# Six transposes of x in a chunked linear-attention and MLP kernel: from DMA to TensorE, with fewer unread matmuls

## The chip, the cores and the metric

The kernel runs on one core of a Trainium2 chip. The metric is device time in microseconds (us) of one execution; for the kernel before it is the median of six executions. A further execution was recorded by the hardware profiler, and all rows shown come from that one.

The engines are named as in the profile: PE (TensorE matmuls), PEld (TensorE weight loads), DVE (VectorE), ACT (ScalarE), POOL (GpSimd) and SP (SyncE, which here only issues DMAs). Each engine works through its own queue in order.

## The reference, cut to what matters

```python
# q, k, v: (4, 8, 768, 64); lam: (8,)
for b in range(nb):                       # blocks of 64 rows
    intra = (qb @ kb.T * Dmask) @ vb      # Dmask[i, j] = lam ** (i - j) for i >= j
    inter = (qb * lam_pow) @ kv_state
    out[block] = intra + inter
    kv_state = lam ** 64 * kv_state + (kb * rev_pow).T @ vb
x = out as (4, 768, 512)                  # the heads side by side
xn = (x - mean) / sqrt(var + 1e-6) * g_ln
result = x + relu(xn @ w_ch1) @ w_ch2     # 512 -> 2048 -> 512
```

Attention with a decay per head and a running state per batch and head, then a normalised two-layer MLP with a residual.

## The kernel before, in words

**Tiles.** The 4 x 768 rows are cut into 12 pairs `u` of two 128-row chunks (`ab` = 0, 1). Pair `u` belongs to batch `u % 4`, so a batch's state passes from pair `u` to pair `u + 4`. The code counts from 0: the "pairs 4 to 6" of the change are `u` = 3, 4, 5, and the "third group" is `g` = 2. Pairs 0 to 5 use `scores`, `kv`, `av`; pairs from 6 on use `scores64`, `kv64`, `av64`, which work in blocks of 64 rows. The MLP works on groups `g`, one per pair, so 256 rows at a time.

**Stages of a pair.** Loads of k, q, v (SP); scaling and casting into `kq` and `vb` (`in_k_one`, `in_q_one`, `in_v`, mostly on POOL); a DMA transpose of `kq` to `kqT` (`transpose_dma`, line 266); scores and masked scores (PE line 282 or 362, DVE line 292 or 368); the state (`kv`, `new_state`, `states64`); the products of masked scores with v (`av`, line 428, or `av64`, line 415); the inter-chunk products (`inter`, line 441), which add to the same two PSUM banks `po0` and `po1`. Halfway through `inter`, `reader` makes DVE (for pairs up to 6) read eight columns of each bank into `seen` (line 452), and the second half of `inter` waits for that.

**From x to the MLP.** `norm(u, ab)` copies x out of `po` (ACT, line 463), takes mean and variance (DVE, lines 465 and 466), and writes the centred and scaled bf16 tile `xc` (DVE, line 470). `to_xT(u, ab)` makes its transpose, a half of the group's `xT`: for pairs 0 and 1 by four PE transposes into a bank of the pool `mm` and an ACT copy (lines 490 and 491), for all others by a DMA transpose on SP's queue (line 486). `rstd_of` makes 1/std (ACT line 496, DVE line 498), which is applied at the very end.

**Units of the MLP.** The MLP is cut into units. An `m1` unit is 8 matmuls of 128x256 (line 530) and one ACT relu of 128x512 into `hT` (line 533). An `m2` unit of groups 0 to 5 is 4 matmuls of 128x512 (line 666); a quarter of a chunk's output, and every fourth is followed by the output's DVE instruction (line 690). For groups 6 to 11 the second layer is done by seven products of half-sized blocks instead of eight (line 565), for which `w_sums` makes sums of weights on DVE (lines 787 to 791). The units lie in one list, `plan`, in order of groups; `units(n)` takes the next n.

**What sets the order.** Nothing is scheduled by a planner: the last 350 lines of the kernel write the order out by hand, attention steps between units, and every engine's queue follows that order. The scheduler that the language offers is switched off (`manual_schedule`), and only semaphores for data and buffers are added.

**PSUM.** All eight banks are given away: four to `mm`, two to `sc`, one each to `po0` and `po1`. A new tile in a bank waits until all readers of the one before it are done.

**Unread matmuls.** In the first `m1` unit of group 2, 20 matmuls of 128x8 into the unit's own bank come first; the unit's real matmuls overwrite them (lines 525 and 526).

```python
        if u >= 2:
            nc.sync.dma_start_transpose(dst, s["xc"][:, ab])
        else:
            xt = mm_tile([128, KA, 128], BF16, "xt")
            for kk in range(KA):
                nc.tensor.transpose(xt[:, kk, :], s["xc"][:, ab, kk * 128:(kk + 1) * 128], ident)
            nc.scalar.copy(dst, xt)
```

Of the kernel before, what the change touches and what calls it, by code (L numbers as in the profile page):

```python
# [8 lines left out]
BF16 = mybir.dt.bfloat16  # L9
# [8 lines left out]
def kernel(  # L18
# [20 lines left out]
    KA = DM // 128  # L39
# [15 lines left out]
    ps = ctx.enter_context(tc.tile_pool(name="ps", bufs=1, space=PSUM))  # L55

    half = [slice(0, 64), slice(64, 128)]
    XB = 3
    LB = 6

    def mm_tile(shape, dtype, name):
        return ps.tile(shape, dtype, tag="mm", bufs=4, name=name)
# [4 lines left out]
    def source(src, u, hs):  # L67
        cc, b = divmod(u, B)
        return src[b, hs, cc * W:(cc + 1) * W, :].rearrange("h (p j) d -> p h (j d)", j=2)

    def fill(got, name, u, hs, eng=None):
        eng = eng or nc.sync
        src = dict(k=k, q=q, v=v)[name]
        if u < LB:
            eng.dma_start(got[:, hs], source(src, u, hs))  # L75
# [11 lines left out]
    def open_in(u, gate):  # L87
        qkv_in[u] = {name: inp.tile([128, H, 2 * D], F32, tag=name + "in", name=name + "in") for name in "kqv"}
        if gate:
            nc.gpsimd.memset(qkv_in[u]["k"][:, 0, 0:1], 0.0)  # L90

    def load_in(u, name, eng):
        got = qkv_in[u][name]
        fill(got, name, u, slice(0, H), eng)
        qkv_in[u][name] = got.rearrange("p h (j d) -> p h j d", j=2)
# [54 lines left out]
    def make_keep64():  # L150
        for dst, base in ((keep64, 0), (keep64_b, D)):
            nc.gpsimd.memset(dst, 1.0)
            nc.gpsimd.affine_select(
                out=dst, in_=dst, compare_op=ALU.is_ge, fill=0.0,
                base=base, pattern=[[1, D]], channel_multiplier=-1,
            )
        nc.vector.tensor_copy(keep64[half[1]], keep64_b[half[1]])
# [49 lines left out]
    def open_window(u):  # L207
        kq = wk.tile([128, 2, NP, 2, 2, D], BF16, tag="kq", bufs=3, name="kq")
        vb = wk.tile([128, H, 2, D], BF16, tag="vb", bufs=4, name="vb")
        st[u] = dict(kq=kq, vb=vb)  # L210
        if u < XB:
            st[u]["kqT"] = wk.tile([128, 2, NP, 2, 128], BF16, tag="kqT", bufs=3, name="kqT")

    def part(a, dst, hs):

        return dst[:, a, hs.start // 2:hs.stop // 2].rearrange("p a j e d -> p a e j d")
# [9 lines left out]
    def in_q(u, eng, hs=ALL):  # L226
        src = qkv_in[u]["q"][:, hs].rearrange("p (a e) j d -> p a e j d", e=2)
        dst = part(1, st[u]["kq"], hs)
        if u < LB:
            lq = lam_q[:, hs, :].rearrange("p (a e) j -> p a e j", e=2)  # L230
# [11 lines left out]
    def in_q_one(u, eng, j):  # L242
        src = qkv_in[u]["q"].rearrange("p (a e) j d -> p a e j d", e=2)
        lq = (lam_q[:, :, j] if u < LB else lam_p[:, 0, :]).rearrange("p (a e) -> p a e", e=2)
        eng.tensor_tensor(part(1, st[u]["kq"], ALL)[:, :, :, j], src[:, :, :, j],  # L245
                          lq[:, :, :, None].to_broadcast([128, NP, 2, D]), op=ALU.mult)

    def in_v(u, eng, hs=ALL):
        n = hs.stop - hs.start
        lv = lam_v[:, hs, :, None] if u < LB else lam_p[:, 1, hs, None, None]  # L250
        eng.tensor_tensor(st[u]["vb"][:, hs], qkv_in[u]["v"][:, hs], lv.to_broadcast([128, n, 2, D]), op=ALU.mult)  # L251
# [167 lines left out]
    def av(u, pairs, chunks=(0, 1)):  # L419
        s = st[u]  # L420
        if "po" not in s:
            s["po"] = [ps.tile([128, H, D], F32, tag=f"po{ab}", name=f"po{ab}") for ab in range(2)]
        for p in pairs:
            for e in range(2):
                for j in range(2):
                    for jq in range(2):
                        for ab in chunks:
                            nc.tensor.matmul(s["po"][ab][half[jq], 2 * p + e, :],  # L428
                                             lhsT=s[f"mA{p // 2}"][half[ab], e, p % 2, j, half[jq]],
                                             rhs=s["vb"][half[ab], 2 * p + e, j],  # L430
                                             start=(p == 0 and e == 0 and j == 0), stop=False, skip_group_check=True)
# [45 lines left out]
    def to_xT(u, ab):  # L477
        s = st[u]
        t = 2 * u + ab
        g = group_of[t]  # L480
        i = t - groups[g][0]
        if i == 0:
            xT_of[g] = gp.tile([128, KA, GT * 128], BF16, tag="xT", bufs=3, name="xT")
        dst = xT_of[g][:, :, i * 128:(i + 1) * 128]
        if u >= 2:
            nc.sync.dma_start_transpose(dst, s["xc"][:, ab])
        else:
            xt = mm_tile([128, KA, 128], BF16, "xt")
            for kk in range(KA):
                nc.tensor.transpose(xt[:, kk, :], s["xc"][:, ab, kk * 128:(kk + 1) * 128], ident)  # L490
            nc.scalar.copy(dst, xt)

    def rstd_of(u):
        s = st[u]
        std = wk.tile([128, 2], F32, tag="std", name="std")
        nc.scalar.activation(std, s["mv"][:, :, 1], ACT.Sqrt, bias=eps_t, scale=XS * XS)
        rstd = xp.tile([128, 2], F32, tag="rstd", name="rstd")
        nc.vector.reciprocal(rstd, std)
        x_keep[u] = (s["x"], rstd)
# [13 lines left out]
    def mlp(g):  # L513
# [6 lines left out]
        def m1(u):  # L520
            nonlocal hT
            if hT is None:
                hT = gp.tile([128, KB, GT * 128], F16, tag="hT", bufs=2, name="hT")
            pm = mm_tile([128, NB, N], F32, "pm1")
            for _ in range(20 if (g, u) == (2, 0) else 0):
                nc.tensor.matmul(pm[0:8, 0, 0:8], lhsT=fill_in, rhs=fill_in, start=True, stop=True, skip_group_check=True)
            for b in range(NB):
                n = u * NB + b
                for kk in range(KA):
                    nc.tensor.matmul(pm[:, b, :], lhsT=w1[n // W2K][:, kk, (n % W2K) * 128:(n % W2K + 1) * 128],  # L530
                                     rhs=xT_of[g][:, kk, 0:N], start=(b == 0 and kk == 0),
                                     stop=(b == NB - 1 and kk == KA - 1), skip_group_check=True)
            nc.scalar.activation(hT[:, u * NB:(u + 1) * NB, 0:N], pm, ACT.Relu)  # L533
# [138 lines left out]
        m2.sums = h_sums  # L672
        m2s[g] = m2
        return m1, m2

    def rows_of(u):

        cc, b = divmod(u, B)
        order = "(c p j) d -> j p c d" if u < LB else "(j c p) d -> j p c d"
        return out[b, cc * W:(cc + 1) * W, :].rearrange(order, c=2, j=2)  # L680
# [15 lines left out]
    def store(u):  # L696
        for j in range(2):
            nc.sync.dma_start(rows_of(u)[j], o_of[u][half[j]])
# [82 lines left out]
    def w_sums(c, n):  # L781
        v = w2[c].rearrange("p (k e) d -> p k e d", e=2)
        w = DM // 2
        b11, b12, b21, b22 = v[:, :, 0, 0:w], v[:, :, 0, w:], v[:, :, 1, 0:w], v[:, :, 1, w:]
        t1, t2, t3, t4 = (wt[c][:, :, i] for i in range(4))
        if n == 0:
            nc.vector.tensor_tensor(t1, b12, b11, op=ALU.subtract)
            nc.vector.tensor_tensor(t3, b12, b22, op=ALU.add)
        else:
            nc.vector.tensor_tensor(t2, b11, t3, op=ALU.subtract)  # L790
            nc.vector.tensor_tensor(t4, t2, b21, op=ALU.add)
# [28 lines left out]
    def s1(u):  # L820
        kv(u)
        scores(u, 0)
        new_state(u, 0, nc.gpsimd)
        mask(u, 0, (0,))
        new_state(u, 1, nc.gpsimd)
        mask(u, 0, (1,))

    def wind_up(u):


        s = st[u]
        if u < LB:
            av(u, range(NP))
# [45 lines left out]
    def s4(u):  # L879
        inter(u, 1)  # L880
        if st[u]["S"][0][1] is not None:
            norm(u, 0)
        norm(u, 1)

    def p4(u):
        to_xT(u, 0)
        to_xT(u, 1)
# [27 lines left out]
    def X2(u):  # L915
        scores64(u)
        inter(u - 1, 1)
        mask64(u, 0)
        norm(u - 1, 0)
        norm(u - 1, 1)  # L920
        mask64(u, 1)

    def X(u):

        if u - 1 < LB:
            av(u - 1, range(NP))
        else:
            av64(u - 1)
        inter(u - 1, 0)
        kv64(u)  # L930
        scores64(u)
        inter(u - 1, 1)
        states64(u, 0)
        mask64(u, 0)
        states64(u, 1)
        norm(u - 1, 0)
        norm(u - 1, 1)
        mask64(u, 1)
# [89 lines left out]
    def units(n):  # L1028
        for _ in range(n):
            f, *a = next(steps)  # L1030
            f(*a)
# [60 lines left out]
    s3(3)  # L1092
    units(1)
    s4(3)
    to_xT(3, 0)
    to_xT(3, 1)
    open_in(6, False)
    load_in(6, "k", nc.sync)
    units(1)
# [3 lines left out]
    units(2)  # L1103
    rstd_of(3)
    make_keep64()
    units(3)
    store(2)
    transpose_dma(5, 0)
    transpose_dma(5, 1)
# [14 lines left out]
    s3(4)  # L1124
    units(2)
    s4(4)
    to_xT(4, 0)
    to_xT(4, 1)
    load_in(7, "q", nc.sync)
    units(2)  # L1130
    transpose_dma(6, 0)
    transpose_dma(6, 1)
    load_in(7, "v", nc.sync)
    units(4)
    s1(5)
    rstd_of(4)
    open_window(7)
# [16 lines left out]
    load_in(8, "k", nc.sync)  # L1154
    units(2)
    X2(6)
    to_xT(5, 0)
    to_xT(5, 1)
    in_v(7, nc.gpsimd)
    load_in(8, "q", nc.sync)  # L1160
    load_in(8, "v", nc.sync)
# [5 lines left out]
    w_sums(1, 0)  # L1167
    rstd_of(5)
    units(1)
    w_sums(1, 1)  # L1170
    units(4)
    X(7)
    store(4)
# [166 lines left out]
```

## Time and profile before

| What | us |
|---|---|
| median of six executions | 212.37 |
| lowest and highest of them | 211.62 and 214.89 |
| the profiled execution's own time | 213.04 |
| its span, from its first to its last instruction | 211.3 |
| PE busy in the span | 199.7 |
| DVE, ACT, POOL busy | 139.6, 98.0, 83.2 |
| share of the 16 DMA engines' span on the queue that SP fills | 74.3% |

The span of 211.3 us and the 1.7 us around it make the profiled execution's 213.04 us. All positions below are us from the span's start. Rows of instruction groups give line, engine, operation, the tiles written and read (out<-in), the count, then busy time and the mean duration of one. The duration of a matmul is longer than the distance to the next one's start, since matmuls overlap in the array; where the text counts PE time, it takes distances between starts.

### The profile page before, as it was taken

The numbers are of one execution on the slowest core, as the hardware profiler recorded it, in microseconds if no ns is written. First come the engines' busy times: TensorE is split into PE (matmuls) and PEld (weight loads), VectorE is DVE, ScalarE is ACT, GpSimd is POOL, SyncE is SP. The second block draws the span as 40 slices with busy tenths as digits, with TensorE's granted clock in tenths as the row PEclk, the third lists the DMA queues.
The fourth block names the chain that finished last, engine by engine and source line by source line (L and its number), as shares of the span: only waits on it lengthen the run. The fifth ranks groups of instructions, "written<-read, shape, count | busy, mean of one in ns | idle before, by whom it ended". The sixth has DMA issues, their size and how long they took to land.

```text
span 211.3 us, 7148 instructions
## 1 busy us (share of the span) xinstructions
PE 199.7 (94%) x3079; PEld 151.2 (72%) x3079; DVE 139.6 (66%) x293; ACT 98.0 (46%) x195; POOL 83.2 (39%) x113
## 2 busy tenths in 40 slices
PE   2988997999999999999999999999999999999992
PEld 1477786644685476487477488888888888888881
DVE  2577652448556464755997589899797887876253
ACT  3855878411154055237057067185284372661630
POOL 4647318519837174208237055273192202011020
PEclk9999999999999999999999999999999999999998
DMA  3999999999999999999989899898948950430303
GB/s 104 299 270 214 167 245 192 201 305 287 172 296 269 131 228 205 177 175 247 203 187 243 152 225 150 173 199 145 163 76 165 285 128 3 103 50 0 99 16 87
DMA packets 94305, 37.17 MB, mean 176 GB/s; under 512 B 68417, under 2 KB 91457, under 8 KB 94274
## 3 DMA queue, kind: packets, MB, share of 16 engines
q1 hardware_dynamic: 89664, 32.32, 74.3%
q0 software_dynamic: 4224, 4.19, 12.7%
q8 instruction: 24, 0.39, 0.8%
q10 hardware_dynamic: 386, 0.20, 0.4%
q14 instruction: 7, 0.06, 0.1%
HBM read 27.27 MB, written 6.29 MB: 159 GB/s over the span
## 4 chain that ended last, share of the span: by engine, by line
PE 61%; issue 13%; DMA 13%; DVE 5%; POOL 3%; SPq 2%; ACT 1%; POOLq 0%; DVEq 0%; ACTq 0%
PE pm L530 28%; PE pm L666 17%; DMA w<-in_moe_w_ch_dram 5%; DMA qin<-in_q_dram 4%; PE pwa L565 3%; DMA kin<-in_k_dram 3%; PE pwd L565 2%; PE pwc L565 2%; SPq L75 2%; PE po L441 1%; PE sc L282 1%; PE pwb L565 1%; PE po L428 1%; POOL o L590 1%; POOL kq L245 1%
## 5 line engine op out<-in xcount | busy, mean ns | idle before, releaser
L530 PE MATMUL pm<-xT,w 128*128 128x256 bf16 x736 | 85.0, 273 | 0.1
L530 PEld LDWEIGHTS <-w 128*128 128x128 bf16 x736 | 70.0, 98 | 9.6 <-issue 0.6
L533 ACT ACTIVATE hT<-pm 128x512 f16<-128x512 f32 x92 | 55.1, 599 | 40.1 <-PE pm L530 39.4
L666 PE MATMUL pm<-w,hT 128*128 128x512 f16 x192 | 43.3, 379 | 0.0
L666 PEld LDWEIGHTS <-hT 128*128 128x128 f16 x192 | 18.2, 98 | 20.5
L322 POOL TENSOR_TENSOR Sn<-Stmp,lam_s 128x256 bf16<-128x256 f32 x16 | 9.8, 612 | 53.4 <-DVE Stmp L400 34.6
L565 PEld LDWEIGHTS <-hs 128*128 128x128 f16 x192 | 18.7, 98 | 2.2
L292 DVE TENSOR_TENSOR mA<-sc,keep 128x512 bf16<-128x512 f32 x20 | 13.1, 682 | 8.3 <-PE sc L282 8.3
L470 DVE SCALAR_TENSOR_TENSOR xc<-po,mv,g_row 128x512 bf16<-128x512 f32 (+1 forms) x24 | 16.8, 706 | 1.8
L463 ACT COPY x<-po 128x512 f32<-128x512 f32 x18 | 9.9, 588 | 15.7 <-PE po L441 10.4
L565 PEld LDWEIGHTS <-hT 128*128 128x128 f16 x144 | 13.6, 98 | 2.7 <-ACT hT L533 1.2
L590 POOL TENSOR_TENSOR o<-ev_u,x 128x256 f32<-128x256 f32 x4 | 3.1, 782 | 31.5 <-ACT ev_u L589 31.5
L548 DVE TENSOR_TENSOR hs<-hT 128x1024 f16<-128x1024 f16 x12 | 10.4, 865 | 6.9 <-ACT hT L533 6.9
L465 DVE BATCH_NORM_STATS2 stats<-x 128x6 f32<-128x512 f32 x18 | 12.4, 686 | 3.8 <-ACT x L463 3.7
L245 POOL TENSOR_TENSOR kq<-qin,lam_q 128x512 bf16<-128x512 f32 x10 | 10.3, 1045 | 8.1 <-DMA qin<-in_q_dram 8.1
L690 DVE SCALAR_TENSOR_TENSOR o<-pm,rstd,x 128x512 f32<-128x512 f32 x12 | 8.8, 743 | 6.9 <-PE pm L666 6.9
L251 POOL TENSOR_TENSOR vb<-vin,lam_v 128x1024 bf16<-128x1024 f32 (+1 forms) x7 | 11.6, 1660 | 2.5 <-DMA vin<-in_v_dram 1.6
L251 POOL TENSOR_TENSOR vb<-vin,lam_p 128x1024 bf16<-128x1024 f32 x6 | 11.4, 1897 | 2.8 <-DMA vin<-in_v_dram 2.7
L245 POOL TENSOR_TENSOR kq<-qin,lam_p 128x512 bf16<-128x512 f32 x12 | 12.3, 1042 | 0.2
L452 ACT COPY seen<-po 128x8 f32<-128x8 f32 x8 | 1.0, 166 | 17.5 <-PE po L441 17.5
L368 DVE TENSOR_TENSOR mA<-sc,keep 128x512 bf16<-128x512 f32 x12 | 8.2, 680 | 1.4 <-PE sc L362 1.4
L259 PE MATMUL tp<-ident,kq 128*128 128x128 bf16 x48 | 6.2, 265 | 1.7 <-DVE kq L240 0.8
(139 smaller groups left out, 265.4 us busy)
## 6 DMA issues: line engine op xcount, KB each, us to landing
out_dram<-o SPq DMA_DIRECT2D x18, 256.0 KB, 4.9
w<-in_moe_w_ch_dram POOLq DMA_DIRECT2D x8, 512.0 KB, 9.1
kin<-in_k_dram SPq DMA_DIRECT2D x14, 256.0 KB, 4.9
qin<-in_q_dram SPq DMA_DIRECT2D x14, 256.0 KB, 4.7
vin<-in_v_dram SPq DMA_DIRECT2D x14, 256.0 KB, 5.2
kin<-in_k_dram SPq DMA_DIRECT2D x5, 512.0 KB, 7.1
qin<-in_q_dram SPq DMA_DIRECT2D x5, 512.0 KB, 9.1
vin<-in_v_dram SPq DMA_DIRECT2D x5, 512.0 KB, 8.7
```

The source lines that it names most:

```text
L245: eng.tensor_tensor(part(1, st[u]["kq"], ALL)[:, :, :, j], src[:, :, :, j], lq[:, :, :, None].to_broadcast([128, NP, 2, D]), op=ALU.mult)
L251: eng.tensor_tensor(st[u]["vb"][:, hs], qkv_in[u]["v"][:, hs], lv.to_broadcast([128, n, 2, D]), op=ALU.mult)
L292: nc.vector.tensor_tensor(s[f"mA{hf}"][:, e], s[f"sc{hf}"][e], kp[:, None, :, :].to_broadcast([128, 2, 2, 128]), op=ALU.mult)
L322: eng.tensor_tensor(dst, src, lam_s[:, :, None].to_broadcast([128, NP, D]), op=ALU.mult)
L463: nc.scalar.copy(x, po)
L465: nc.vector.bn_stats(stats, po if early else x)
L470: nc.vector.scalar_tensor_tensor(xc[:, sl], in0=po[:, sl], scalar=mv[:, 0:1], in1=g_row[:, sl], op0=ALU.subtract, op1=ALU.mult)
L530: nc.tensor.matmul(pm[:, b, :], lhsT=w1[n // W2K][:, kk, (n % W2K) * 128:(n % W2K + 1) * 128], rhs=xT_of[g][:, kk, 0:N], start=(b == 0 and ...
L533: nc.scalar.activation(hT[:, u * NB:(u + 1) * NB, 0:N], pm, ACT.Relu)
L548: nc.vector.tensor_tensor(s13, b[:, :, 1:2, :].to_broadcast([128, n, 2, 128]), b[:, :, 0:4:3, :], op=ALU.subtract)
L565: nc.tensor.matmul(pr[bank], lhsT=lhs(r), rhs=rhs, start=(first and r == 0), stop=(r == KB // 2 - 1), skip_group_check=True)
L666: nc.tensor.matmul(acc[i], lhsT=hT[:, kk, i * 128:(i + 1) * 128], rhs=w2[kk // W2K][:, kk % W2K, :], start=(kk == 0), stop=(kk == KB - 1))
```

## The change

Three things change.

1. `to_xT` for `u` = 3, 4, 5 no longer issues a DMA transpose on SP. It makes four PE transposes into a bf16 tile that takes the bank `po{ab}` (the bank of the same pair's `av` and `inter` products, free once `norm` has read it), and an ACT copy from there to `xT`.
2. The calls of `to_xT` for these pairs move to later places in the hand-written order. For `u` = 3 they go from just behind `s4(3)` to places with four and five more units ahead of them; for `u` = 4 the same, with four and five units of the six that lie between `s4(4)` and `s1(5)`; for `u` = 5 both go behind the fifth of nine units between `X2(6)` and `X(7)`, with `w_sums(1, 1)` between them.
3. The unread matmuls ahead of group 2 go from 20 to 4.

```diff
     XB = 3
+    X_PE = (3, 4, 5)
     LB = 6
...
-        if u >= 2:
+        if u >= 2 and u not in X_PE:
             nc.sync.dma_start_transpose(dst, s["xc"][:, ab])
         else:
-            xt = mm_tile([128, KA, 128], BF16, "xt")
+            if u < 2:
+                xt = mm_tile([128, KA, 128], BF16, "xt")
+            else:
+                xt = ps.tile([128, KA, 128], BF16, tag=f"po{ab}", name="xt")
             for kk in range(KA):
                 nc.tensor.transpose(xt[:, kk, :], s["xc"][:, ab, kk * 128:(kk + 1) * 128], ident)
             nc.scalar.copy(dst, xt)
...
-            for _ in range(20 if (g, u) == (2, 0) else 0):
+            for _ in range(4 if (g, u) == (2, 0) else 0):
...
     s4(3)
-    to_xT(3, 0)
-    to_xT(3, 1)
     open_in(6, False)
     load_in(6, "k", nc.sync)
     units(1)
...
     make_keep64()
-    units(3)
+    to_xT(3, 0)
+    units(1)
+    to_xT(3, 1)
+    units(2)
     store(2)
...
     s4(4)
-    to_xT(4, 0)
-    to_xT(4, 1)
     load_in(7, "q", nc.sync)
     units(2)
     transpose_dma(6, 0)
     transpose_dma(6, 1)
     load_in(7, "v", nc.sync)
-    units(4)
+    units(2)
+    to_xT(4, 0)
+    units(1)
+    to_xT(4, 1)
+    units(1)
     s1(5)
...
     X2(6)
-    to_xT(5, 0)
-    to_xT(5, 1)
     in_v(7, nc.gpsimd)
...
     rstd_of(5)
     units(1)
+    to_xT(5, 0)
     w_sums(1, 1)
+    to_xT(5, 1)
     units(4)
     X(7)
```

## The prediction

> **What bounds the kernel now.** I read the page's busy rows by slices first, then the same by stretches of 4 us, then PE's waits.
>
> ```profile
> PE 199.7 (94%) x3079; PEld 151.2 (72%) x3079; DVE 139.6 (66%) x293; ACT 98.0 (46%) x195; POOL 83.2 (39%) x113
> ...
> PE   2988997999999999999999999999999999999992
> ...
> PEclk9999999999999999999999999999999999999998
> ```
>
> From the eighth slice (37 us) to the last but one PE is full and its clock is granted whole. The stretches say how full: between 36 and 204 us only three of 4 us are below 4.00 busy, and the two that lose most are
>
> ```profile
> 72.00:76.00 4.00, 3.91 (x75) 2.79 (x73) 2.49 (x5) 1.19 (x2) 0.82 (x2) 1.00 0.90 183
> 104.00:108.00 4.00, 3.73 (x140) 2.24 (x139) 3.89 (x12) 0.00 (x0) 0.00 (x0) 1.00 0.92 175
> ```
>
> (first number after the window's length: PE busy). So added PE work is paid in full unless it falls into one of PE's few waits, and DMA relief pays only where PE waits for a DMA. The chain of waits agrees: from 36 us on it is nearly all PE. I therefore looked for PE's losses by distances between matmul starts, since modelled ends hide short ones.
>
> **Added: 24 PE transposes.** Pairs 0 and 1 already do this. PE's timeline has one set of four in a dense stretch, and one early set:
>
> ```profile
> 18.13 0.63 PE L490 MATMUL xt<-ident,xc 128*128 128x128 bf16 x4
> 18.56 0.30 PE L259 MATMUL tp<-ident,kq 128*128 128x128 bf16 x1
> ...
> 27.72 0.39 PE L490 MATMUL xt<-ident,xc 128*128 128x128 bf16 x4
> 27.95 1.04 PE L530 MATMUL pm<-xT,w 128*128 128x256 bf16 x8
> ```
>
> 27.95 - 27.72 = 0.23 us for four, 56 ns each with finer digits, no loss on either side. The early set takes 18.56 - 18.13 = 0.43 us, 107 ns each, soon after PE had sat idle. I take 56 ns, because the six sets lie between units in the full region, as at 27.72: 6 x 4 x 0.056 = **+1.34 us**. The other end is 24 x 0.107 = 2.57 us. The Trainium skill, "TensorE: Matmul & The Clock Gate", section "Part 4: PE-mode transpose", speaks against this change: it gives about 275 ns for one in a kernel and says that transposes do not count towards the full clock. The row's durations (219 to 314 ns) look like that figure, but the starts at 27.72 are 56 ns apart. Charged by the page, the sets would cost 24 x 0.275 = 6.6 us, an estimate that I don't use.
>
> Do these sets wait for their input? xc of pair 3 is done at 67.60 and 69.27 (line 470 starts at 66.85 and 68.52, 0.75 each). PE reaches the new places after four units of 0.864 us from 66.36, at 69.82, and at 70.91: no wait. Pair 4: xc is done at 84.15 and 85.82, PE arrives at 84.90 and 85.99, a margin of 0.17 us. Pair 5: xc at 100.79 and 102.46, PE at 102.61 and 102.83, a margin of 0.37. The bank is free with xc, its last reader. Behind a waiting transpose the next unit would be queued, so a late xc would cost PE its whole lateness.
>
> Added on ACT: six copies of 0.58 us (line 491). ACT is idle in those places: 69 to 73 us, 83.4 to 90 but for one 0.3 us instruction, 102 to 108. Pair 3's second copy ends near 71.13 + 0.2 + 0.58 = 71.9 and group 3's first matmul comes at 72.86: covered by two units. Without that cover it is at most 0.58 us a copy. The bank's next users, `av` at 78.6, 93.1 and 106.2, come over 1.5 us after the copies.
>
> **Removed: six DMA transposes on SP.** Each took 1.2 to 1.7 us of SP's queue. Behind them stand loads of pairs 6, 7 and 8, and `kqT` transposes from pair 5 on, which come up to 3 us earlier each; POOL's queue issues none of it. PE waits for none of these now (pair 5's `kqT` lands at 86.7, its scores start at 87.0), so earlier is worth nothing here. What pays is PE's own wait for xT. At group 3's first unit:
>
> ```profile
> 70.69 1.89 PE L666 MATMUL pm<-w,hT 128*128 128x512 f16 x8
> 72.67 0.60 PE L530 MATMUL pm<-xT,w 128*128 128x256 bf16 x4
> ```
>
> Eight matmuls at 0.216 end their turn at 70.69 + 1.73 = 72.42; the next starts at 72.67. Pair 3's second DMA transpose was issued at 70.1 and the first of them took 3.6 us to land, so this is the wait for xT. It goes: **-0.25 us**. Groups 4 and 5 start at 90.4 and 107.9 without such a wait (transposes issued at 87.0 and 104.4, landed at 89.9 and 106.9): 0.
>
> **Moved onto a wait: pair 5.** At the `seen` fence of X(7) PE waits for DVE:
>
> ```profile
> 97.76 0.45 PE L362 MATMUL sc<-kqT 64*64 64x64 bf16 x32
> 98.03 0.30 PE L441 MATMUL po<-Sn,kqT 64*64 64x64 bf16 x16
> ```
> ```profile
> 106.85 0.50 PE L362 MATMUL sc<-kqT 64*64 64x64 bf16 x32
> ...
> 107.61 0.19 PE L441 MATMUL po<-Sn,kqT 64*64 64x64 bf16 x1 [0.27 <-DVE seen L452]
> ```
>
> The same 32 matmuls hold PE for 0.27 us in one place and 0.76 in the other: some 0.45 to 0.49 lost. In the chain of waits DVE is busy from 99.04 (norm of pair 5) to 107.5 with no break over 0.3 us, so its `seen` comes at a fixed time after pair 5's inter product, whatever PE does meanwhile. The new eight transposes (0.45 us) lie in just that stretch, so PE arrives later at a fence that doesn't move: **-0.45 us**, pair 5 is free. The tightest point is DVE's output instruction at 106.74, whose matmuls end at 106.22 and would end at 106.67.
>
> Pair 4's eight find no wait (PE has none from 76.8 to 98 us) and are paid: 0.45 us, in the 1.34 already.
>
> **Removed: 16 unread matmuls.**
>
> ```profile
> 47.63 7.94 PE L666 MATMUL pm<-w,hT 128*128 128x512 f16 x36
> 55.50 0.64 PE L526 MATMUL pm<-fill_in 128*8 128x8 bf16 x20
> 56.08 3.67 PE L530 MATMUL pm<-xT,w 128*128 128x256 bf16 x32
> ```
> ```profile
> L486 SPq DMA_TRANSPOSE xT<-xc x2: 1207/2147/3087, 49.6 to 52.8; - x2
> ...
> DMA to landing us min/median/max: 3.2/4.5/5.9
> ```
>
> Twenty take 0.58 us with the switch behind them, about 25 ns each, so 16 are 0.40 us on paper. But pair 2, whose transposes stay DMAs, lands at 49.6 + 5.9 = 55.5 and 52.8 + 3.2 = 56.0, and the real matmuls need both (the other way round, the second would land at 58.7, after its readers' start): they start at 56.08 now and could hardly start before 56.0. The unread matmuls stand where PE would wait. I take 0, with 0.07 (the switch) likely and 0.40 the end if the DMA lands early. Nothing ahead of 55 us changes, so it should not. The wait that appears is 0.4 us; at 107 us PE lost as much and ran on at 109 ns a 128x256 matmul, so I charge nothing for the clock.
>
> **Sum.** 1.34 - 0.25 - 0.45 - 0 = **+0.64 us**. Against the profiled execution: 213.04 + 0.64 = 213.68 (span 211.3 to 212.0). That execution lies 0.67 above the median of 212.37; I carry the difference over: **213.0 us**, +0.3%. A measurement of this kernel tells about 0.5% (1.06 us) from no change, so the forecast is "within".
>
> **Rivals.**
> 1. Slower: the transposes run at the early set's spacing. If 128x512 matmuls beside them, or weight loads of xc that can't be pulled ahead, space them at 107 ns, the sum is 2.57 - 0.70 = +1.87, 214.2 us. It decides "slower" from (1.06 + 0.70) / 24 = 73 ns on. For: line 259's transposes have a median of 82 ns over all. Against: the sets at 27.72 and 36.0 in dense stretches go at 56. 0.15.
> 2. The fence of X(7) moves with PE, because DVE's output instructions wait for the later matmuls, or SP's earlier loads shift POOL and DVE work. Then pair 5 costs its 0.45: +1.09, 213.5 us, on the border. The 0.07 us margin speaks for it. 0.20.
> 3. Relief of the DMA queues does more: xT of pair 2 lands early (-0.40), and the 0.27 us that PE loses within the scores at 76.1 goes. Then +0.64 - 0.67 = -0.03, 212.3 us. For it: SP's queue is issuing almost without a break from 64 to 83 us. Against: the order ahead of 55 us is the same, and the wait at 76.1 is DVE's. 0.15.
> 4. The change doesn't do what it says, in part: this is the unread matmuls, whose removal shortens nothing. It is in the forecast.
>
> **How the numbers follow.** Forecast 0.50, rivals 0.15, 0.20, 0.15. For faster by over 0.5% PE would have to save 1.7 us beyond the sum, and all its waits from 57 to 201 us that I can find come to under 1.1; 0.07 is left for scatter and what I don't see. Slower: rival 1 whole, half of rival 2, a little of the forecast: 0.27. Within: 0.66. The range goes from rival 3 less 0.4 for scatter to rival 1: 211.9 to 214.2.
>
> **What would show it.** The 24 transposes at line 490 with starts 56 ns apart; the matmul behind group 2's last units still starting at about 56.0, after four unread ones and an idle 0.4; no loss ahead of group 3's first unit; the `seen` wait at X(7) gone or under 0.1; pair 4's stretch longer by 0.45. PE waits at line 490 for line 470 would make it wrong upwards, an earlier landing of pair 2's xT downwards.

## The result, and the profile after

The changed kernel takes 213.97 us (median of 38 executions, 212.47 to 215.43). The kernel before was timed again beside it and the experiments: 213.25 us over 78 executions, not the 212.37 of the first six. The ratio is 1.0045, 95% interval 1.0028 to 1.0062: **slower by 0.95 us, between 0.6 and 1.3.** The ratio leaves out executions more than 1.5% above the fastest of their kernel, 14 of the 78 before and none of the 38 after; over all executions the medians lie 0.72 us apart and the means 0.50. The profiled execution takes 214.14 us, its span is 212.4 us.

The same stretches of 4 us as before (PE busy is the first number behind the length):

```profile
72.00:76.00 4.00, 4.00 (x75) 2.82 (x73) 1.99 (x4) 1.00 (x3) 0.61 (x1) 1.00 1.36 229
104.00:108.00 4.00, 4.00 (x62) 1.93 (x61) 3.90 (x12) 1.07 (x2) 0.00 (x0) 1.00 1.20 233
```

Both holes are closed: 3.91 and 3.73 have become 4.00. The view of PE's waits from 57 to 201 us, which had one row, is empty. Yet the span is longer, because what fills the holes is new work. PE's timeline at group 2 and at group 3 (start, length, then the group):

```profile
55.74 0.24 PE L530 MATMUL pm<-fill_in 128*8 128x8 bf16 x4
56.39 0.83 PE L534 MATMUL pm<-xT,w 128*128 128x256 bf16 x6 [0.40 <-DMA xT<-xc]
```
```profile
70.13 0.39 PE L494 MATMUL xt<-ident,xc 128*128 128x128 bf16 x4
70.35 1.03 PE L670 MATMUL pm<-w,hT 128*128 128x512 f16 x4
71.22 0.39 PE L494 MATMUL xt<-ident,xc 128*128 128x128 bf16 x4
71.44 1.89 PE L670 MATMUL pm<-w,hT 128*128 128x512 f16 x8
73.17 1.04 PE L534 MATMUL pm<-xT,w 128*128 128x256 bf16 x8
```

Sixteen unread matmuls are gone and the first real matmul comes 0.65 us behind the first unread one, where it was 0.58: PE idles instead and waits for pair 2's xT. At group 3 each set of four transposes holds PE for 70.35 - 70.13 = 0.22 us, 56 ns each. Eight matmuls at 0.216 from 71.44 end at 73.17, just where group 3 starts: that wait is gone. Pair 4's two sets:

```profile
85.41 0.39 PE L494 MATMUL xt<-ident,xc 128*128 128x128 bf16 x4
85.64 1.03 PE L670 MATMUL pm<-w,hT 128*128 128x512 f16 x4
86.50 0.39 PE L494 MATMUL xt<-ident,xc 128*128 128x128 bf16 x4
86.72 1.03 PE L670 MATMUL pm<-w,hT 128*128 128x512 f16 x4
```

They hold PE for 0.23 and 0.22 us, and no wait was there to take them. Pair 5's stretch and the fence of X(7):

```profile
99.35 1.05 PE L534 MATMUL pm<-xT,w 128*128 128x256 bf16 x8
...
103.69 0.61 PE L494 MATMUL xt<-ident,xc 128*128 128x128 bf16 x8
104.14 3.62 PE L670 MATMUL pm<-w,hT 128*128 128x512 f16 x16
107.68 0.45 PE L416 MATMUL po<-vb,mA 64*64 64x64 bf16 x32
108.08 0.47 PE L382 MATMUL pk<-vb,kq 64*64 64x64 bf16 x32
108.38 0.50 PE L363 MATMUL sc<-kqT 64*64 64x64 bf16 x32
109.03 0.39 PE L534 MATMUL pm<-xT,w 128*128 128x256 bf16 x2
```

The same two matmuls of line 530 (now 534) in the kernel before, the first behind pair 5's inter products and the first of group 5:

```profile
98.27 0.50 PE L530 MATMUL pm<-xT,w 128*128 128x256 bf16 x3
...
107.93 0.28 PE L530 MATMUL pm<-xT,w 128*128 128x256 bf16 x1
```

Eight transposes take 0.45 us, and from line 363's start to group 5 it is now 0.65 us where it was 107.93 - 106.85 = 1.08. From the end of pair 5's inter products to group 5's first matmul it is 109.03 - 99.35 = 9.68 us; before, 107.93 - 98.27 = 9.66.

**Steps.** What single executions do ahead of group 2 differs by more than the change (group 2 starts between 54.5 and 58.0 us in the 20 profiles of this study, with much the same program up to there). So I compare distances between the first matmuls of groups, read from PE's timeline, in us:

| kernel | first unread matmul to group 2 | group 2 to 3 | 3 to 4 | 4 to 5 | 5 to PE's last matmul |
|---|---|---|---|---|---|
| before | 0.58 | 16.59 | 17.70 | 17.56 | 99.16 |
| after | 0.65 | 16.78 | 18.16 | 17.70 | 99.16 |
| transposes_only | 1.00 | 16.78 | 18.16 | 17.58 | 99.18 |
| after_again | 0.29 | 16.78 | 18.29 | 17.62 | 99.08 |

After against before: 0.07 + 0.19 + 0.46 + 0.14 = 0.86 us. The first column is the least certain: with 4 unread matmuls there it lies between 0.2 and 1.5 us over eight profiles, by when pair 2's xT lands. And before has one profile only; five profiles of kernels that move or drop unread matmuls alone take 151.5 to 153.0 us from group 2 to PE's last matmul, where before took 151.00 and after 151.80. That steps and time agree so well is in part luck.

### The profile page after: what moved, and what is told of

It reads as the page before. It is cut to its first block, busy times and chain, and to the rows that moved or that the text cites. A ratio compares the mean times of both kernels' runs of the same rounds, so it can differ in the third digit from the quotient of the medians.

```text
span 212.4 us, 7155 instructions
## 1 busy us (share of the span) xinstructions
PE 201.5 (95%) x3087; PEld 154.0 (72%) x3087; DVE 137.9 (65%) x293; ACT 100.9 (47%) x201; POOL 82.7 (39%) x113
## 4 chain that ended last, share of the span: by engine, by line
PE 66%; issue 12%; DMA 9%; DVE 4%; SPq 3%; POOL 3%; ACT 1%; POOLq 0%; DVEq 0%; ACTq 0%
PE pm L534 30%; PE pm L670 16%; DMA vin<-in_v_dram 7%; SPq L76 3%; PE pwa L569 3%; PE pwc L569 2%; PE pwd L569 2%; DMA xT<-xc 2%; PE po L429 2%; PE po L442 2%; PE sc L283 1%; PE pwb L569 1%; POOL o L594 1%; DVE xc L471 1%; PE sc L363 1%
## 5 line engine op out<-in xcount | busy, mean ns | idle before, releaser
L670 PE MATMUL pm<-w,hT 128*128 128x512 f16 x192 | 44.1, 379 | 0.0
L552 DVE TENSOR_TENSOR hs<-hT 128x1024 f16<-128x1024 f16 x12 | 9.6, 803 | 7.0 <-ACT hT L537 7.0
L246 POOL TENSOR_TENSOR kq<-qin,lam_q 128x512 bf16<-128x512 f32 x10 | 10.3, 1045 | 8.1 <-DMA qin<-in_q_dram 8.1
L495 ACT COPY xT<-xt 128x512 bf16<-128x512 bf16 x10 | 5.7, 585 | 7.1 <-PE xt L494 7.1
```

The lines of the kernel that those rows point to most:

```text
L552: nc.vector.tensor_tensor(s13, b[:, :, 1:2, :].to_broadcast([128, n, 2, 128]), b[:, :, 0:4:3, :], op=ALU.subtract)
L670: nc.tensor.matmul(acc[i], lhsT=hT[:, kk, i * 128:(i + 1) * 128], rhs=w2[kk // W2K][:, kk % W2K, :], start=(kk == 0), stop=(kk == KB - 1))
```

## The experiments

Theory: PE is the bound; the transposes cost 56 ns each, less what falls into PE's waits, and the unread matmuls cost nothing where they stand. Rivals: the unread matmuls matter themselves; the waits would go anyway or come back elsewhere; a TensorE stop that belongs to none of these. The ratios are against the kernel before on the same chip in the same set of runs, with their intervals.

**The unread matmuls alone.**

```diff
-            for _ in range(20 if (g, u) == (2, 0) else 0):
+            for _ in range(4 if (g, u) == (2, 0) else 0):
```

> The kernel before with 4 unread matmuls in place of 20 and nothing else. If they only stand where TensorE waits for pair 2's xT: the time stays (-0.07 to +0.1 us), the first real matmul of group 2 still starts 0.5 to 0.65 us behind the first unread one, with 0.4 us of it idle. Rival, that they are paid work: 0.40 us faster, the real matmuls start 0.2 us behind the first unread one. Rival, that they keep the clock up: slower by 0.5 us or more, with matmuls of 128x256 further apart than 109 ns behind the wait.

1.0074 (1.0046 to 1.0102): slower, as no theory of a mere wait has it. PE's timeline at group 2:

```profile
55.09 0.24 PE L526 MATMUL pm<-fill_in 128*8 128x8 bf16 x4
56.59 1.16 PE L530 MATMUL pm<-xT,w 128*128 128x256 bf16 x9 [1.26 <-DMA xT<-xc]
```

The wait is 1.26 us here, because pair 2's xT landed at 56.5 while PE was early; twenty unread matmuls would have covered half a microsecond of it and shortened nothing. Group 2 to 5 takes as long as before (51.89 us against 51.85). The loss lies behind 121 us: 0.35 us of waiting for pair 8's kqT, and two stops of 0.67 and 0.88 us. Was that this program's, or chance?

> The kernel before with 4 unread matmuls in place of 20, a second time. If its +0.74% comes from stops of TensorE that belong to this program (its instructions reach TensorE by DMA in blocks of 16 KB, and the stops without a waited-for semaphore at 153 and 170 us stand near such fetches): again about +1.5 us, with stops of 0.3 to 0.9 us at the same matmuls in the profile. If it was chance: within 0.5 us of before and no stops there.

0.9996 (0.9961 to 1.0031) the second time: the two intervals do not meet. But the largest stop is at the same matmul again. So I moved the unread matmuls, and then the whole instruction stream, apart from each other:

```diff
                 acc[i] = mm_tile([128, DM], F32, "pm2")
+                for _ in range(16 if (g, i) == (1, 1) else 0):
+                    nc.tensor.matmul(acc[i][0:8, 0:8], lhsT=fill_in, rhs=fill_in, start=True, stop=True, skip_group_check=True)
```

> The kernel before with 4 unread matmuls at group 2's first unit, and 16 more of the same kind ahead of the last output chunk's matmuls of group 1, some 3.5 us earlier, so that from 56 us on every TensorE instruction has the place in the instruction stream that it has before. If the place in the stream makes the stops: the same as before (-0.1 to +0.3 us) and no stops at 123, 153 and 170 us. If the unread matmuls are needed at the wait itself: +1.5 us as with 4 alone.

> The kernel before with 16 of its 20 unread matmuls moved 3.5 us ahead, a second time; it was timed 0.5% below before. By the theory of steps it is the kernel before: 1.000, and the first time was scatter. If the place of the unread matmuls matters: 0.995 again.

0.9950 (0.9918 to 0.9983), then 0.9989 (0.9950 to 1.0028). With 4 unread matmuls at the wait and 16 earlier, the kernel is no slower than before: nothing needs them at the wait. In its timeline the 16 hold PE for 0.48 us, and group 2 then starts without a wait for xT:

```profile
50.29 0.54 PE L666 MATMUL pm<-fill_in 128*8 128x8 bf16 x16
50.77 3.63 PE L668 MATMUL pm<-w,hT 128*128 128x512 f16 x16
54.33 0.24 PE L526 MATMUL pm<-fill_in 128*8 128x8 bf16 x4
54.50 0.72 PE L530 MATMUL pm<-xT,w 128*128 128x256 bf16 x5
```

The first of these two profiles loses 0.80 us at 131 us, which I did not expect; the second loses nothing there. It is a wait for DVE's `hs` (line 548):

```profile
130.21 0.60 PE L565 MATMUL pwc<-wt,hs 128*128 128x256 f16 x4
130.25 1.14 DVE L548 TENSOR_TENSOR hs<-hT 128x1024 f16<-128x1024 f16 x1
131.44 0.61 PE L565 MATMUL pwc<-wt,hs 128*128 128x256 f16 x4 [0.64 <-DVE hs L548]
```

DVE's instruction ends at 131.39 and PE goes on at 131.44. In the kernel before it took 0.67 us:

```profile
131.66 0.67 DVE L548 TENSOR_TENSOR hs<-hT 128x1024 f16<-128x1024 f16 x1
```

The next run tests the place in the instruction stream.

```diff
-    unread(16)
+    unread(8)
     nc.tensor.matmul(g_all, lhsT=ones, rhs=g_one, start=True, stop=True)
-    unread(16)
+    unread(8)
```

> The kernel before with all 20 unread matmuls at group 2, but 16 instead of 32 unread ones in its first 7 us: from there on every TensorE instruction comes 32 places earlier in the stream, as in the kernel with 4. If the place in the stream makes the stops: slower by about 1.5 us, with stops at the same matmuls as with 4 (behind 121 us). If the unread matmuls at group 2 matter themselves: the same as before within 0.4 us.

1.0061 (1.0033 to 1.0089), with all 20 unread matmuls at group 2. PE's timelines behind X(11): fills4_only, fills4_again, shift32_at_start, and the kernel before.

```profile
168.46 1.59 PE L530 MATMUL pm<-xT,w 128*128 128x256 bf16 x13
170.77 0.94 PE L530 MATMUL pm<-xT,w 128*128 128x256 bf16 x7 [0.71 <-issue]
```
```profile
167.45 1.59 PE L530 MATMUL pm<-xT,w 128*128 128x256 bf16 x13
169.69 1.05 PE L530 MATMUL pm<-xT,w 128*128 128x256 bf16 x8 [0.65 <-issue]
```
```profile
168.20 1.59 PE L530 MATMUL pm<-xT,w 128*128 128x256 bf16 x13
170.41 0.83 PE L530 MATMUL pm<-xT,w 128*128 128x256 bf16 x6 [0.62 <-issue]
```
```profile
166.84 3.34 PE L530 MATMUL pm<-xT,w 128*128 128x256 bf16 x29
```

Three times PE stops behind the same 13th matmul, for 0.8 to 0.9 us by distances of starts, and "issue" says that nothing in the profile made it wait. All three have their TensorE instructions 32 places earlier in the stream than before. None of the 16 profiles with other shifts has the stop, but pair2_kv4 (24 places earlier) has one of 0.53 us four matmuls sooner, behind the 9th: with a weight load for each matmul, that is the same count of TensorE instructions from the start. So place in the stream matters, and the unread matmuls do not. It is not all of the timing: the larger loss in shift32_at_start is at X(8), a 1.46 us wait for pair 8's kqT.

**The transposes alone.** The changed kernel with 20 unread matmuls.

> The changed kernel with its 20 unread matmuls back: the six transposes alone. Sum of the prediction: +0.64 us against before (1.34 paid, 0.25 back at group 3, 0.45 back at the fence of X(7)). If the measured +0.95 (interval 0.6 to 1.3) comes from the transposes, this is within 0.1 us of the changed kernel; if it comes from the fewer unread matmuls, this is 0.3 us or more below it.

1.0062 (1.0026 to 1.0098). The steps in the table above are 0.19 + 0.46 + 0.02 = 0.67 us over before; the prediction's sum was 0.64. Its first column, 1.00, is again a late xT of pair 2. By time it can't be told from the changed kernel, whose interval lies inside this one: the transposes carry the change.

**One pair at a time.** In each, `X_PE` holds one pair and only that pair's calls of `to_xT` move.

> The kernel before with pair u=5 alone moved to TensorE, 20 unread matmuls. Theory: its 0.45 us fall into the wait for DVE at the fence of X(7), time +0.0 us (within 0.15); the distance from the end of pair 5's inter products to group 5's first matmul stays at 9.66 us within 0.05. Rival, that the fence moves with TensorE: +0.45 us and that distance is 10.1 us.

1.0022 (0.9984 to 1.0061), and 106.79 - 97.12 = 9.67 us, 9.66 before: free, as predicted. PE's timeline shows the 0.45 us and the fence with no wait behind line 363:

```profile
97.12 1.05 PE L534 MATMUL pm<-xT,w 128*128 128x256 bf16 x8
...
101.46 0.61 PE L494 MATMUL xt<-ident,xc 128*128 128x128 bf16 x8
101.91 3.62 PE L670 MATMUL pm<-w,hT 128*128 128x512 f16 x16
...
106.15 0.50 PE L363 MATMUL sc<-kqT 64*64 64x64 bf16 x32
106.79 0.61 PE L534 MATMUL pm<-xT,w 128*128 128x256 bf16 x4
```

> The kernel before with pair u=4 alone moved to TensorE, 20 unread matmuls. Theory: no wait is there to take it, +0.45 us; the distance from group 3's first matmul to that of group 4 (17.7 us before) grows by 0.45 us. Rival, that shorter DMA queues give back as much: 0.0 us.

1.0031 (0.9990 to 1.0072); group 3 to 4 takes 18.30 us, 0.60 more than before. 0.45 is the transposes; 0.13 of the rest is lost in pair 4's inter products, at no row of a wait. after_again loses 0.10 there too (18.29), after and transposes_only do not (18.16). This profile also waits 0.77 us at 134 us for DVE's `hs`, as fills4_pad16 does.

> The kernel before with pair u=3 alone moved to TensorE, 20 unread matmuls. Theory: 0.45 us paid and the 0.25 us wait for xT at group 3's first unit gone, +0.2 us; from the first matmul of the second layer's units behind pair 3's inter products to group 3's first matmul 6.31 us before, 6.5 us here. Rival, that the wait is not one for xT: it stays, 6.75 us, +0.45 us.

1.0053 (1.0018 to 1.0088); 73.37 - 66.87 = 6.50 us, as the theory has it. Its profile loses a further 0.78 us at 134 us, in the same wait for DVE's `hs` as fills4_pad16, which moves no transpose; so I don't count it as the pair's.

**The waits alone.** Two waits can be filled without any transpose.

```diff
-    w_sums(1, 1)
     units(4)
     X(7)
+    w_sums(1, 1)
```

> The kernel before with w_sums(1, 1) behind X(7) in place of ahead of it: no transposes on TensorE. Two DVE instructions of 0.42 us leave the chain that the fence of X(7) waits for. Theory: the wait of 0.45 us goes, time -0.45 us; the distance from pair 5's inter products to group 5's first matmul goes from 9.66 to 9.2 us. Rival, that DVE falls behind later instead and the wait comes back at X(8): 0.0 us.

By distance 106.16 - 96.97 = 9.19 us, 0.47 gone, and the wait does not come back at X(8): the row of PE's waits is empty. By time 1.0008 (0.9971 to 1.0044), no change clear of the noise.

> The changed kernel with w_sums(1, 1) behind X(7). Theory: the transposes of pair 5 already fill the wait, so there is nothing left for this move to gain: the same time as the changed kernel within 0.1 us (+0.6 to +0.95 us against before), although the same move makes the kernel before 0.45 us faster. Rival, that the two savings are independent: 0.45 us below the changed kernel.

1.0056 (1.0023 to 1.0090), within the interval of the changed kernel; from pair 5's inter products to group 5 it is 107.93 - 98.30 = 9.63 us against 9.68. What gains 0.47 us before gains 0.05 here: the wait could be filled once.

```diff
     transpose_dma(5, 1)
+    kv(4)
+    new_state(4, 0, nc.gpsimd)
     units(1)
-    s1(4)
+    scores(4, 0)
+    mask(4, 0, (0,))
+    new_state(4, 1, nc.gpsimd)
+    mask(4, 0, (1,))
```

> The kernel before with w_sums(1, 1) behind X(7), and with kv(4) and the first state of pair 4 ahead of group 3's first unit in place of behind it: work of 0.27 us where TensorE waits for pair 3's xT. Theory: both waits go, -0.45 and -0.25 us: 0.7 us faster than before, without any transpose moved; perhaps 0.2 us more, since DVE and POOL begin pair 4's states earlier and the 0.27 us stop within its second scores is theirs. Rival, that xT then lands later against the queue: -0.45 us only.

> The kernel before with w_sums(1, 1) behind X(7) and kv(4) ahead of group 3's first unit, a second time. By steps it gained 0.69 us between group 2 and the last matmul. If steps tell the time: 0.996 to 0.998. If the gain is lost elsewhere: 1.000 as at the first time.

0.9996 (0.9956 to 1.0037) and 0.9997 (0.9958 to 1.0036). From group 2 to PE's last matmul the first profile is 150.35 us against 151.00, a gain of 0.65; the second 150.82, having lost 0.45 to a wait for pair 8's kqT. In time neither shows.

**Further tries for a faster kernel, and the size of the change.** pair2_kv4 puts `X_PE = (2,)` and no unread matmul at group 2 on top of sums_kv4; the aligned one adds 12 unread matmuls at the start.

> As sums_kv4, and pair u=2 (the one whose xT TensorE waits for at group 2, 0.2 to 1.5 us in the profiles) on TensorE with no unread matmul there. Theory: eight transposes for 0.45 us in place of 0.58 us and more of unread matmuls and waiting, -0.15 to -0.9 us by execution, with the other two moves -1.0 us against before (0.995). Its instructions stand 24 places earlier behind 55 us, so a stop of 0.8 us by place could take most of that back: then 0.999.

> As pair2_kv4, with 12 more unread matmuls in the first 7 us, so that behind 55 us all TensorE instructions have the places in the stream that they have before. Theory: no stop behind 120 us and -1.0 us (0.995), 0.3 us less where the early unread matmuls are on the path. If places in the stream don't matter: as pair2_kv4, 0.3 us above it at most.

1.0021 (0.9976 to 1.0066) and 1.0002 (0.9964 to 1.0039): no gain. PE comes earlier to data that come no earlier. PE's waits of the aligned kernel from 57 to 201 us:

```profile
PE pm L534 <- DMA xT<-xc: 2.0, 1, 2.0
```

Pair 5's xT, issued at 105.5, landed at 109.6, and group 5 stood waiting. In pair2_kv4 the same happens at X(8), with 1.4 us for pair 8's kqT.

> The kernel before with pair u=5 alone on TensorE (free by its place, as in pair5_only) and kv(4) ahead of group 3's first unit. In pair2_kv4_aligned, where TensorE came earlier to group 5, its first matmul waited 2.2 us for pair 5's xT by DMA; here no DMA makes that xT. Theory: the 0.25 us at group 3 and the 0.27 us within pair 4's scores go and nothing comes back: -0.5 us (0.9975), and no wait at group 5. Rival, that the queue of DMAs bounds these groups and hands the wait on: 1.000, with a new wait at the scores of pair 7 or 8 (107 or 122 us).

0.9948 (0.9911 to 0.9986): apart from the first timing of fills4_pad16, which did not come again, the one version that was timed faster than both kernels. Its profile doesn't explain it: that execution is among its longest (214.59 us, median 212.0), waits 0.8 us for pair 3's xT at group 3 and 0.4 for pair 5's kqT. One of 18 comparisons with its interval's end 0.14% below one is a candidate, not a finding.

> The changed kernel with 24 instead of 32 unread matmuls in its first 7 us, so that behind 103 us its TensorE instructions have the places in the stream that they have before (they stand 16 places later in the changed kernel). If part of the measured +0.95 us is stops by place in the stream: the sum of the prediction remains, +0.6 to +0.75 us against before. If not: +0.95 us as the changed kernel. The difference is near what the rounds can tell; the steps between groups in the profile tell more.

1.0013 (0.9981 to 1.0046), steps as in the changed kernel, no stop. This neither shows nor excludes that part of the change's size is place in the stream.

> The changed kernel unchanged, on the same chip as the next three. The sum by steps of its first profile is +0.8 us (0.07 at the unread matmuls, 0.19 at group 3, 0.46 at pair 4, 0.14 at pair 5), the prediction's +0.64. If that is the whole cause: 1.003 to 1.004 and the same steps again within 0.1 us. If stops by place in the instruction stream add to it in some executions: 1.004 to 1.006, perhaps a stop of 0.8 us near 133 us in the profile.

1.0031 (0.9995 to 1.0066), no stop.

## Why the prediction was right and wrong

- **Time.** 213.97 lies in the range, 0.97 above the forecast. 0.88 of that is the base: six executions gave 212.37, seventy-eight gave 213.25. From the larger base the same sum gives 213.89.
- **Forecast "within".** This failed. The sum was +0.64 us, on the slower side, and I called it no change because I took 0.5% (1.06 us) for what a measurement can tell, a figure that no run stood behind. With 38 executions against 78 the interval is 0.17% (0.36 us) to either side, and 0.95 us lies clear of it. The mechanism and the sign stood in the sum; the step that failed is the size of that resolution, and with it "the forecast is 'within'".
- **24 transposes at 56 ns: +1.34 us.** Right: 0.22 us for each set in every place, 0.45 for the double set. The rival at 107 ns is out, and its 107 was the clock: in the trace of before, transposes of lines 259 and 490 mostly start 106 to 107 ns apart up to 18.6 us and 55 to 57 ns apart from 19.3 us on, and the trace's clock record grants 1.00 from 18.73 us on (ahead of the first record the views print 1.00 for want of one). The median of 82 ns that spoke for the rival is a mixture of the two. The Trainium skill, "TensorE: Matmul & The Clock Gate", "Part 4: PE-mode transpose", gives about 275 ns for one; the distance between starts is a fifth of that here. By the clock record of the changed kernel 1.00 is granted from 23.1 us on, through all six sets, so that section's other remark, that the full clock doesn't engage for transposes, does not show in sets this short.
- **Pair 3's wait, -0.25 us.** Right for the profile it was read from: +0.19 us from group 2 to 3 is 0.45 - 0.25. But the wait is that execution's. Where pair 3 stays with the DMA and no work of pair 4 moves ahead of group 3, group 2 to 3 takes 16.33 us in four of nine profiles, with no wait to win back, and up to 16.92 in the others; with pair 3 on TensorE it takes 16.78 in all six.
- **Pair 5 free.** Right, 9.66 to 9.68 us. The rival that the fence moves is out; sums_later and after_sums_later show that the place was a wait for DVE that can be filled once.
- **Pair 4 paid.** Right: 0.46.
- **Unread matmuls, 0.** Right in kind: PE waits for pair 2's xT instead, 0.07 us longer in the profile, 0.3 us shorter in after_again and 0.8 longer in after_sums_later. What I didn't foresee is that a count of instructions that do nothing shifts all that follow.
- **Mis-sized.** The sum's zero at group 4 to 5 measured 0.14: 0.12 of it lies in X1(6) (pair 5's products and pair 6's states), where three places of the small matmuls take longer and no row has a wait. pair4_only and after_again lose 0.13 and 0.10 in another such place. That cause stays open. So 0.86 us by steps against 0.64; both lie in the measured interval of 0.6 to 1.3, and the rest, if there is one, isn't located.
- **DMA relief.** Worth 0.25 us in the profile of before, as predicted, but DMA arrival varies: PE waited for a DMA behind group 2 in 10 of the 15 profiles that make xT of pairs 3 to 5 by DMA, in whole or in part (0.25 to 2.2 us at a time), and not once for 0.15 us or more behind 58 us in the five that make all three on PE. The five take 151.70 to 151.81 us from group 2 to PE's last matmul, the others 150.35 to 153.00. The change buys evenness for its 1.34 us, and not enough of it.
- **A reading that was too round.** "From 36 us on it is nearly all PE" does not hold for the chain of waits: ACT and then DVE have it from 98.4 to 107.6 us, as the prediction itself uses, and from 175 us on it runs through ACT, POOL and "issue". PE's starts carry the sum, so nothing in it changes.

## What to carry to other kernels

Where one engine is full, work moved onto it costs its start-to-start time unless it lands in one of that engine's own waits; find these by distances between starts, and count each wait once. Filler ahead of a data wait showed no cost here, and removing it gained nothing. A forecast near zero should be put against what the timing will resolve, not against a round bound, and its base taken from more than six executions.

## What the runs showed of the hardware

**TensorE stopped for 0.5 to 0.9 us with no semaphore waited for, at fixed places in the instruction stream.** The 20 profiles have five such stops behind group 2: the three shown above, the one in pair2_kv4, and the one of 0.67 us at 153.7 us in fills4_only. Counted by the traces' records of TensorE's queue, 5,314 records come ahead of the matmul that ends the stop in four of them, and 4,802 in the fifth, which is 512 fewer. The page lists a queue that carries instructions:

```profile
q8 instruction: 24, 0.39, 0.8%
```

24 packets, 0.39 MB, 16 KB each: 0.39 MB over PE's some 6,170 instructions is 64 bytes an instruction, so these look like PE's, a packet holds 256 of them, and 512 are two packets. By the traces' DMA records the last packet ahead of a stop ended 1.3 to 1.5 us before the stop did. At the same two places of the stream without a stop it ended 1.5 to 6.6 us before. So the stops stand where a late instruction packet would put them. No run moved a packet, and the profile has no row for such a wait: likely by that, and not shown.

The 0.77 to 0.80 us that fills4_pad16, pair3_only and pair4_only lose at 131 to 134 us are of another kind. They are waits for DVE's `hs`, whose instruction took 1.14 to 1.15 us in these three and 0.67 to 0.69 in the other 17 profiles. Why it took longer stays open.

**The clock is a part of the scatter of the start.** By the clock records of the traces 1.00 is first granted between 17.8 and 23.2 us in 19 of the 20 profiles, and at 10.3 us in sums_kv4_again. In three it falls back once: for 3.4 us at 25 us in sums_kv4 and after_again, and from 13.7 to 20.5 us in sums_kv4_again. A stretch of the first sums_kv4 (PEclk is the third number from the end), PE's timeline in it, and the same matmuls in before:

```profile
24.70:28.10 3.40, 3.40 (x46) 2.50 (x46) 0.17 (x1) 1.71 (x6) 0.02 (x1) 0.50 1.08 191
```
```profile
24.61 0.62 PE L316 MATMUL pk<-vb,kq 64*64 64x64 bf16 x32 [2.31 <-POOL vb L251]
25.16 3.33 PE L530 MATMUL pm<-xT,w 128*128 128x256 bf16 x16
```
```profile
22.62 0.45 PE L316 MATMUL pk<-vb,kq 64*64 64x64 bf16 x32 [0.41 <-POOL vb L251]
23.00 1.92 PE L530 MATMUL pm<-xT,w 128*128 128x256 bf16 x16
```

The fall comes behind a wait of 2.31 us for POOL's `vb` (1.94 in after_again, 0.41 in before), and at the half clock the 16 matmuls take 3.33 us instead of 1.92. Group 2 then starts at 58.0 us instead of 56.1, by the wait and the clock together. The Trainium skill, "TensorE: Matmul & The Clock Gate", "Part 1: The HAM clock gate (the "warmup" mystery)", tells of two clock states and a free-running window of about 3.4 us, so that the moment of the change differs from run to run. The half rate and the 3.4 us agree with these rows.
